# Two products on one array: moving the buffers that TensorE reads to other offsets modulo 256 bytes

## The chip, the cores and the metric

The kernel runs on one core of one Trainium2 chip. Its time is the device time of one launch in microseconds (us); the figure for the kernel before is the median of three runs. TensorE is called PE in the profile, VectorE DVE, ScalarE ACT, GpSimd POOL and SyncE SP; "PEld" is TensorE's loading of weights, which the profile lists as an engine of its own. A *pair* below is two matmuls that run at once on the two 64-row halves of TensorE's array.

## The reference

```
xn  = layernorm(x)                       # x: 2048 x 576, float32
qkv = xn @ wqkv                          # 32 heads of 18
A   = sliding dilated attention (8 keys, 2 apart) @ wo
h   = maximum(xn @ w1, 0)                # 576 -> 4608
B   = h @ w2                             # 4608 -> 576
out = x + A + B
```

All products are kept close to float32: each operand is split into a high part in the float32r format and the rest ("hi" and "lo"), and three of the four partial products are added up (hi·hi, hi·lo, lo·hi).

## The kernel before

The 2048 rows are taken in two phases of 1024, each phase in four blocks of 256 rows (NTB), and the 4608 hidden columns in 36 strips of 128, three to a chunk. One *slot* is one strip for one block, and the loop at L826 walks through 288 of them. A slot does three things on TensorE:

- **The first product** (`h_two`, L577): two slots' hidden strips are computed together, half of their terms in each of the two slots. Per slot 14 pairs of 256 columns run through `mm_rows` (L118, instruction line L125). The *weights*, the operand that is loaded into the array, are strips of the tile `w1t`; the *moving* operand, which streams through, is the transposed input `xT`. The profile names the group `ph<-xT,w1t` or `pm<-xT,w1t` by the PSUM tile that it fills.
- **q, k and v** (`qkv_tile`, L378) in 64 of the slots: 14 pairs of 432 columns, weights `xT`, moving `wq`.
- **The second product** (`o_two`, L603): 12 pairs, four sets of three. The weights are the two halves of `hhi` and `hlo`, the split hidden strip that ACT (L559) and DVE (L562) made from the first product two slots earlier; the moving operand is `w2t`, in a cut of 256 columns and one of 320 (`CUT`, L68), because one PSUM bank holds 512 columns and the product has 576. The order of a slot is 3 pairs of 256, 3 of 320, 3 of 256, 3 of 320. A set takes hi with w2's high part, hi with w2's low part, and lo with w2's high part. In eight slots the product with `wo` rides along, with weights `k` and `xn` and moving `wq` and `v`, which then hold wo.

The weights of a pair are loaded while the pair before it streams, so at nearly every moment two reads of SBUF run beside each other: the moving operand of this pair and the weights of the next.

The order of the work is written out by hand. A planner (`t["pe"]`, `t["dve"]`, L112) adds up estimated TensorE and VectorE time as instructions are issued, and `run_bg` (L498) lets attention's VectorE operations into a slot only while the VectorE estimate is not ahead. `two` (L157) makes the hi and lo parts of a weight tile: one ACT copy (L158) and one DVE subtraction (L162), with DVE's estimate raised by (columns + 70) / 960 us. The tiles of w2 are split in `w2_task` (L184) from a staging buffer `st` that SP fills by DMA.

Where a buffer lies is set by the order of the pools (L75 to L91) and their sizes: each takes the next free bytes of every partition, rounded up to 32. The first tile starts 128 bytes past a multiple of 256 in the built program. From there the offsets follow by addition: `x` is 2304 bytes, `xT` 10240, `qo` 20480, `k` and `v` 8640 each, `w1t` 5120, `w2t` 4608, `wq` 17280, `st` 2560, `hhi` and `hlo` 1024, `pr` 4608, `xn` 2560. The pool `gap` at L85 holds 192 unused bytes. The results are in the table of the section on the change.

Of the kernel before, what the change touches and what calls it, by code (L numbers as in the profile page):

```python
# [10 lines left out]
F32 = mybir.dt.float32  # L11
F32R = mybir.dt.float32r
# [6 lines left out]
P = 128  # L19
# [37 lines left out]
def tile_body(ctx: ExitStack, tc: tile.TileContext, x, wqkv, wo, w1, w2, out):  # L57
    nc = tc.nc
    S, D = x.shape
# [6 lines left out]
    DR = D - KT * P  # L66
    D2 = D // 2
    CUT = (slice(0, 256), slice(256, D))  # L68
    scale = Dh ** -0.5
    SPC = NTB * C  # L70
    SPP = NCH * SPC

    ctx.enter_context(tc.manual_schedule())
    pool = lambda name, bufs, **k: ctx.enter_context(tc.tile_pool(name=name, bufs=bufs, **k))
    consts = pool("consts", 1)  # L75
    xp = pool("xp", 11)
    xtp = pool("xtp", NTB)
# [1 line left out]
    kp = pool("kp", 1)  # L79
    vp = pool("vp", 2)  # L80
    w1p = pool("w1p", C + 1)
    w2p = pool("w2p", C + 1)
    wqp = pool("wqp", 1)
    stp = pool("stp", 5)
    gap = pool("gap", 1)  # L85
    gap.tile([P, 48], F32, name="gap")
    hp = pool("hp", LAG + 1)
    prp = pool("prp", 2)
    lgp = pool("lgp", 1)
    smp = pool("smp", 2)  # L90
    tmp = pool("tmp", 2)  # L91
    ps_o = pool("ps_o", 4, space=PSUM)
    ps_h = pool("ps_h", 2, space=PSUM)
# [20 lines left out]
    def mm(o, l, r, start, stop, n):  # L114
        nc.tensor.matmul(o, l, r, start=start, stop=stop)  # L115
        t["pe"] += n / 2400.0 + 0.002

    def mm_rows(runs, behind=None):  # L118


        if behind is not None:
            tc.add_manual_dep(nc.tensor.nop().ins, behind.ins.name, SYNC, reason="PSUM banks change rows")
        for pair in zip(*runs, strict=True):
            for z, (o, l, r, start, stop, n) in zip((slice(0, 64), slice(64, P)), pair):
                ins = nc.tensor.matmul(o, l[z], r[z], start=start, stop=stop)  # L125
            t["pe"] += pair[0][5] * 17 / 16 / 2400.0 + 0.001
        return ins

    def dve(n):
        t["dve"] += (n + 70) / 960.0  # L130
# [6 lines left out]
    def split_task(step, load, split):  # L137
        tasks.append((step, load, split))
# [18 lines left out]
    def two(hi, lo, src, n):  # L157
        nc.scalar.activation(hi, src, AF.Copy)  # L158
        if step_now in by_pool:
            nc.gpsimd.tensor_tensor(lo, src, f32(hi), op=ALU.subtract)  # L160
        else:
            nc.vector.tensor_tensor(lo, src, f32(hi), op=ALU.subtract)  # L162
            dve(n)
# [20 lines left out]
    def w2_task(step, key, f):  # L184
        def load(st):
            nc.sync.dma_start(st[:, 0:D], w2[f * P : (f + 1) * P, :])

        def split(st):
            w = w2p.tile([P, 2, D], F32R, name="w2t")
            two(w[:, 0, :], w[:, 1, :], st[:, 0:D], D)  # L190
            W2[key] = w

        split_task(step, load, split)
# [335 lines left out]
    def wo_run(ph, i, h, terms, upper):  # L529

        r, d = OT[ph, i]
        row = [r[:, j] for j in range(KT)] + [r[:, KT] if upper else d[:, KT]] + [d[:, j] for j in range(KT + 1)]
        return [(row[a], WO[ph][b][:, CUT[h]]) for a, b in terms]


    slots = [(ph, c, tb, f) for ph in range(NPH) for c in range(NCH) for tb in range(NTB) for f in range(C)]
    H, PO = {}, {}
# [60 lines left out]
    def o_tiles(n):  # L598
        for h, c in enumerate(CUT):
            for k in range(2):  # L600
                PO[k, h] = ps_o.tile([P, 512], F32, name="po")[:, 0 : c.stop - c.start]

    def o_two(n):  # L603


        ph, c, tb, f = slots[n]
        hi, lo = H.pop(n)
        w = W2[ph, c, f]
        with_wo = c == WO_CHUNK and f == C - 1
        if f == 0:  # L610
            o_tiles(n)

        def run(k, h, upper):
            cs, first = slice(k * P, (k + 1) * P), k == upper
            z = [(l[:, cs], w[:, b, CUT[h]]) for l, b in ((hi, 0), (hi, 1), (lo, 0))]
            if with_wo:
                more = wo_run(ph, 2 * tb + k, h, (UPPER_MORE if upper else LOWER_MORE) if first else (UPPER if upper else LOWER), upper)
                z = z + more
            return [
                (PO[k, h], l, r, f == 0 and first and j == 0, f == C - 1 and not first and j == len(z) - 1, CUT[h].stop - CUT[h].start)  # L620
                for j, (l, r) in enumerate(z)
            ]

        for j in range(4):
            k, h = divmod(j, 2)
            behind = PB[j - 2] if j > 1 else PB[3] if j == 0 and f else None
            PB[j] = mm_rows((run(k, h, False), run(1 - k, h, True)), behind)
        if with_wo:
            for k in range(2):
                OT.pop((ph, 2 * tb + k))  # L630
        o_out(n, rows=True)
# [3 lines left out]
    def o_mm(n, out=True, which=range(2)):  # L635
        ph, c, tb, f = slots[n]
        hi, lo = H[n]
        w = W2[ph, c, f]
        end = n == len(slots) - 1
        if f == 0 and 0 in which:  # L640
            o_tiles(n)
        for k in which:
            cs = slice(k * P, (k + 1) * P)
            terms = [(j, l, b, h) for j, (l, b) in enumerate(((hi, 0), (hi, 1), (lo, 0))) for h in range(2)]
            if end:
                terms.sort(key=lambda z: -z[3])
            for j, l, b, h in terms:
                mm(
                    PO[k, h], l[:, cs], w[:, b, CUT[h]],
                    f == 0 and j == 0, f == C - 1 and j == 2, D2,  # L650
                )
        if 1 in which:
            H.pop(n)
        if out:
            o_out(n, which)
# [4 lines left out]
    def o_out(n, which=range(2), rows=False):  # L660
        ph, c, tb, f = slots[n]
        if f < C - 1:
            return
        end = n == len(slots) - 1
        t["dve"] = max(t["dve"], t["pe"] - 0.4)
        order = [(k, h) for k in which for h in range(2)]
        if rows:
            order.sort(key=lambda z: z[1])
        elif end:
            order.sort(key=lambda z: (z[0], -z[1]))  # L670
        for k, h in order:
            i = 2 * tb + k
            acc, cols = X[ph, i], CUT[h]
            nc.vector.tensor_tensor(acc[:, cols], PO[k, h], acc[:, cols], op=ALU.add)  # L674
            dve(cols.stop - cols.start)
            if end and k:
                (nc.scalar if h else nc.sync).dma_start(o_v[ph, i][:, cols], acc[:, cols])
            elif end and h == 0:
                store(ph, i)
            elif c == NCH - 1 and h == 1 and not end:  # L680
                at(n + 1, store, ph, i)
# [15 lines left out]
    for ph in range(NPH):  # L697
        b = ph * SPP
# [16 lines left out]
        for i in range(NI):  # L715
            z = b + WO_CHUNK * SPC + C * (i // 2) + C - 1
# [67 lines left out]
    x2[1]()  # L784
    x2[3]()
    o_mm(0)
    o_mm(1)
    make_xt(0, 3, bank=ps_h)
    o_mm(2, out=False)
    stats(0, 4)  # L790
    s5 = stats(0, 5, parts=True)
# [83 lines left out]
```

## Time and profile before

| | |
|---|---|
| median of 3 runs | 1157.87 us (1157.85 to 1158.02) |
| the profiled execution's own time | 1154.82 us |
| its span, first to last instruction | 1153.0 us |
| busy PE / DVE / ACT / POOL | 1145.1 / 795.9 / 295.6 / 53.4 us |
| matmuls | 17334 |
| mean granted TensorE clock | 0.999 |

The span is what the views of the profile show; the execution's own time adds 1.8 us around it. A matmul's duration in the profile is the time from its start to its modelled end, and includes a fixed part in which the next pair is already streaming: a pair of 256 columns lasts 272 ns at the least, while a new one starts about every 113 ns. Of two matmuls of the same shape, the one with the longer duration was held up while it streamed. The views used are the page, the waits of PE, the groups of instructions by shape, the timeline, and the chain of waits.

### The profile page before, as it was taken

The page shows a single profiled execution, that of the slowest core. Times are in us where ns is not written, and L with a number is a line of the kernel's source. Part 1 is how long each engine was busy: PE and PEld are TensorE (multiplying, and loading weights), DVE is VectorE, ACT ScalarE, POOL GpSimd, SP SyncE. Part 2 cuts the span into 40 slices and gives each one's busy share as a digit, 9 for nine tenths or more (in the row PEclk, how much of TensorE's full clock was granted, in tenths as well). Part 3 has the DMA queues.
Part 4 walks back from the last instruction along what each step waited for, and adds up shares of the span by engine and source line. Part 5 has one row for each costly group of instructions (what it writes and reads, how often), then busy time and mean ns, then how long its engine had stood idle before and what let it go on. Part 6 is the DMA issues. An engine that isn't in the chain of part 4 may idle for free.

```text
span 1153.0 us, 38714 instructions
## 1 busy us (share of the span) xinstructions
PE 1145.1 (99%) x17334; PEld 1139.6 (99%) x17334; DVE 795.9 (69%) x1465; ACT 295.6 (26%) x796; POOL 53.4 (5%) x80
## 2 busy tenths in 40 slices
PE   8999999999999999999999999999999999999998
PEld 8999999999999999999999999999999999999998
DVE  7427887877788789643674179868868877896432
ACT  5322221221222221321552122222222212222110
POOL 3200000000000000000110000000000000010000
PEclk9999999999999999999999999999999999999999
DMA  6303312221221311402333033032222304122002
GB/s 186 92 25 85 85 36 66 77 63 51 63 78 32 94 33 46 140 13 56 110 101 97 2 101 87 24 87 64 59 58 53 99 2 113 55 57 76 13 2 84
DMA packets 85238, 76.75 MB, mean 67 GB/s; under 512 B 6624, under 2 KB 68832, under 8 KB 85072
## 3 DMA queue, kind: packets, MB, share of 16 engines
q1 hardware_dynamic: 84640, 73.82, 22.5%
q8 instruction: 136, 2.23, 0.8%
q10 hardware_dynamic: 432, 0.46, 0.1%
q14 instruction: 30, 0.25, 0.1%
HBM read 61.34 MB, written 4.72 MB: 57 GB/s over the span
## 4 chain that ended last, share of the span: by engine, by line
PE 97%; DVE 1%; issue 1%; DMA 1%; ACT 1%; POOL 0%; DVEq 0%; POOLq 0%; ACTq 0%
PE po L125 43%; PE pm L125 27%; PE ph L125 25%; PE pm L354 1%; PE po L115 0%; PE ph L115 0%; DMA x<-in_x 0%; DMA st<-in_w 0%; DMA st<-in_wqkv 0%; DVE bst L263 0%; POOL rstd L270 0%; DVE x L674 0%; ACT xn L283 0%; DVE w2t L162 0%; PE pm L302 0%
## 5 line engine op out<-in xcount | busy, mean ns | idle before, releaser
L125 PE MATMUL po<-w2t,hhi 64*128 64x256 f32 (+1 forms) x4448 | 447.3, 292 | 0.0
L125 PEld LDWEIGHTS po<-w2t,hhi 64*128 64x128 f32 x4448 | 357.6, 185 | 0.5
L125 PE MATMUL po<-w2t,hlo 64*128 64x256 f32 (+1 forms) x2224 | 333.6, 290 | 0.0
L125 PE MATMUL ph<-xT,w1t 64*128 64x256 f32 x5076 | 323.5, 274 | 0.0
L125 PEld LDWEIGHTS ph<-xT,w1t 64*128 64x128 f32 x5076 | 312.5, 184 | 0.1
L674 DVE TENSOR_TENSOR x<-po,x 128x320 f32<-128x320 f32 (+1 forms) x384 | 149.7, 449 | 169.1 <-PE po L125 166.4
L125 PEld LDWEIGHTS po<-w2t,hlo 64*128 64x128 f32 x2224 | 216.6, 185 | 0.0
L125 PE MATMUL pm<-wq,xT 64*128 64x432 f32 x1728 | 179.3, 354 | 0.0
L559 ACT ACTIVATE hhi<-ph 128x256 fp32r<-128x256 f32 x197 | 65.4, 381 | 418.1 <-PE ph L125 409.8
L125 PEld LDWEIGHTS pm<-wq,xT 64*128 64x128 f32 x1728 | 160.1, 184 | 3.2
L125 PE MATMUL pm<-xT,w1t 64*128 64x256 f32 x2430 | 153.5, 273 | 0.0
L125 PEld LDWEIGHTS pm<-xT,w1t 64*128 64x128 f32 x2430 | 148.4, 184 | 0.0
L562 DVE SCALAR_TENSOR_TENSOR hlo<-ph,hhi 128x256 fp32r<-128x256 f32 x197 | 74.5, 417 | 103.4 <-ACT hhi L559 103.1
L439 DVE TENSOR_TENSOR pr<-qo,k 128x1152 f32<-128x1152 f32 x64 | 85.6, 1349 | 4.2 <-DMA k<-k 4.2
L559 ACT ACTIVATE hhi<-pm 128x256 fp32r<-128x256 f32 x91 | 30.0, 382 | 222.6 <-PE pm L125 222.2
L471 DVE TENSOR_TENSOR pr<-lg,v 128x1152 f32<-128x1152 f32 x64 | 84.8, 1349 | 0.3
L442 DVE TENSOR_REDUCE lg<-pr 128x64 f32<-128x1152 f32 x64 | 84.8, 1343 | 0.0
L478 DVE TENSOR_TENSOR pr<-pr 128x288 f32<-128x288 f32 (+1 forms) x128 | 69.9, 598 | 0.0
L562 DVE SCALAR_TENSOR_TENSOR hlo<-pm,hhi 128x256 fp32r<-128x256 f32 x91 | 34.3, 418 | 37.2 <-ACT hhi L559 36.0
L162 DVE TENSOR_TENSOR w2t<-st,w2t 128x576 fp32r<-128x576 f32 x72 | 53.8, 747 | 8.8 <-ACT w2t L158 8.5
L162 DVE TENSOR_TENSOR w1t<-st,w1t 128x640 fp32r<-128x640 f32 x70 | 57.2, 817 | 3.5 <-ACT w1t L158 3.1
L406 ACT ACTIVATE k<-pm 128x144 f32<-128x144 f32 x64 | 19.3, 301 | 146.8 <-PE pm L125 119.5
(86 smaller groups left out, 710.5 us busy)
## 6 DMA issues: line engine op xcount, KB each, us to landing
st<-in_w SPq DMA_DIRECT2D x72, 288.0 KB, 3.1
st<-in_w SPq DMA_DIRECT2D x72, 256.0 KB, 3.0
st<-in_wqkv SPq DMA_DIRECT2D x32, 216.0 KB, 3.0
st<-in_w SPq DMA_DIRECT2D x144, 32.0 KB, 2.7
out<-x SPq DMA_DIRECT2D x15, 288.0 KB, 2.3
x<-in_x SPq DMA_DIRECT2D x14, 288.0 KB, 3.7
k<-k SPq DMA_DIRECT2D x8, 441.0 KB, 3.9
v<-v SPq DMA_DIRECT2D x8, 441.0 KB, 4.9
```

Source lines behind the costliest of these rows:

```text
L125: ins = nc.tensor.matmul(o, l[z], r[z], start=start, stop=stop)
L162: nc.vector.tensor_tensor(lo, src, f32(hi), op=ALU.subtract)
L354: nc.tensor.transpose(pt[:, k], src[rows, k * P : (k + 1) * P], ident[rows, rows])
L406: nc.scalar.activation(k[:, W - 1 + j, :], pq[:, 1, :], AF.Copy)
L439: nc.vector.tensor_tensor(pr[i], q, window(k, i), op=ALU.mult)
L442: nc.vector.tensor_reduce(lg[:, i], pr.pop(i).rearrange(heads, d=Dh), axis=AX.X, op=ALU.add)
L471: nc.vector.tensor_tensor(pr[i].rearrange(heads, d=Dh), e, window(v, i).rearrange(heads, d=Dh), op=ALU.mult)
L478: nc.vector.tensor_tensor(o, z[:, 0:n], z[:, n : 2 * n], op=ALU.add)
L559: nc.scalar.activation(hi, pt, AF.Relu)
L562: nc.vector.scalar_tensor_tensor(lo, pt, 0.0, f32(hi), op0=ALU.max, op1=ALU.subtract)
L674: nc.vector.tensor_tensor(acc[:, cols], PO[k, h], acc[:, cols], op=ALU.add)
```

## The change

It adds empty pools (`space`) so that some buffers move, and stores the tile `w2t` with 16 unused elements (64 bytes) between its columns 0 to 255 and its columns 256 to 575, in rows of 640 elements in place of 576. The high and the low part are therefore made by two calls of `two` per tile, one per cut. The pool `gap` goes.

```diff
+    W2CUT = (slice(0, 256), slice(272, D + 16))
...
+    def space(name, words):
+
+        pool(name, 1).tile([P, words], F32, name=name)
...
     w1p = pool("w1p", C + 1)
+    space("gap_w2", 48)
     w2p = pool("w2p", C + 1)
+    space("gap_wq", 16)
     wqp = pool("wqp", 1)
     stp = pool("stp", 5)
-    gap = pool("gap", 1)
-    gap.tile([P, 48], F32, name="gap")
+    space("gap_h", 32)
     hp = pool("hp", LAG + 1)
     prp = pool("prp", 2)
     lgp = pool("lgp", 1)
     smp = pool("smp", 2)
+    space("gap_tmp", 16)
     tmp = pool("tmp", 2)
...
-            w = w2p.tile([P, 2, D], F32R, name="w2t")
-            two(w[:, 0, :], w[:, 1, :], st[:, 0:D], D)
+            w = w2p.tile([P, 2, 640], F32R, name="w2t")
+            for z, c in zip(W2CUT, CUT):
+                two(w[:, 0, z], w[:, 1, z], st[:, c], c.stop - c.start)
             W2[key] = w
...
-            z = [(l[:, cs], w[:, b, CUT[h]]) for l, b in ((hi, 0), (hi, 1), (lo, 0))]
+            z = [(l[:, cs], w[:, b, W2CUT[h]]) for l, b in ((hi, 0), (hi, 1), (lo, 0))]
...
-                    PO[k, h], l[:, cs], w[:, b, CUT[h]],
+                    PO[k, h], l[:, cs], w[:, b, W2CUT[h]],
```

What TensorE reads, by its start in bytes modulo 256 (every strip, row and cut inside a tile starts at a multiple of 256 from the tile's start, but for the rows of `wq`, 1728 bytes apart, and the second cut of `w2t` after the change, 1088 bytes in):

| pair | moving, before | next weights in the same product, before | moving, after | next weights, after |
|---|---|---|---|---|
| first product, 256 columns | `xT` 192 | `w1t` 0 | 192 | 0 |
| second product, 256 columns | `w2t` 0 | `hhi`, `hlo` 64 | 192 | 0 |
| second product, 320 columns | `w2t` 0 | `hhi`, `hlo` 64 | 0 | 0 |
| q, k, v, 432 columns | `wq` 0, 64, 128 or 192 | `xT` 192 | as before | 192 |
| wo, 256 and 320 columns | `wq` 0 (`v` 64, 128) | `k` 192, `xn` 64 | as before | as before |

Besides these, `pr` and `lg` go from 64 to 0; `st` (128) and `xn` (64) stay where they were modulo 256.

## The prediction

> **What bounds the kernel now.** I read the page first, then who waits for whom on PE, then PE's groups by shape, then the timeline of one slot.
>
> ```profile
> span 1153.0 us, 38714 instructions
> PE 1145.1 (99%) x17334; PEld 1139.6 (99%) x17334; DVE 795.9 (69%) x1465; ACT 295.6 (26%) x796; POOL 53.4 (5%) x80
> PEclk9999999999999999999999999999999999999999
> PE 97%; DVE 1%; issue 1%; DMA 1%; ACT 1%; POOL 0%; DVEq 0%; POOLq 0%; ACTq 0%
> PE po L125 43%; PE pm L125 27%; PE ph L125 25%; PE pm L354 1%; PE po L115 0%; PE ph L115 0%; DMA x<-in_x 0%; DMA st<-in_w 0%; DMA st<-in_wqkv 0%; DVE bst L263 0%; POOL rstd L270 0%; DVE x L674 0%; ACT xn L283 0%; DVE w2t L162 0%; PE pm L302 0%
> ```
>
> TensorE is busy for all of the span, at full clock, and the chain that ended last runs through its pairs at L125, the second product (`po`) with the most, 43%. The waits of PE have five entries:
>
> ```profile
> PE po L106 <- POOL mhalf L101: 1.4, 1, 1.4
> PE pm L302 <- ACT xn L284: 1.2, 1, 1.2
> PE ph L115 <- ACT xT L307: 0.6, 1, 0.6
> PE pm L354 <- DVE xT L343: 0.4, 1, 0.4
> PE pm L302 <- DVE xT L310: 0.3, 1, 0.3
> ```
>
> That is 3.9 us in all, mostly in the start. So only two things move the time by much: how many pairs there are, which the change leaves alone, and how long a pair takes. PE's groups by shape show that this is not set by the number of columns alone (the last number before the second bar is the mean duration in ns):
>
> ```profile
> L125 PE MATMUL ph<-xT,w1t 64*128 64x256 f32 x5076 | 323.5, 274 | 0.0
> L125 PE MATMUL po<-w2t,hhi 64*128 64x320 f32 x2224 | 256.4, 306 | 0.0
> L125 PE MATMUL po<-w2t,hhi 64*128 64x256 f32 x2224 | 226.3, 278 | 0.0
> L125 PE MATMUL pm<-wq,xT 64*128 64x432 f32 x1728 | 179.3, 354 | 0.0
> L125 PE MATMUL po<-w2t,hlo 64*128 64x320 f32 x1112 | 174.3, 304 | 0.0
> L125 PE MATMUL po<-w2t,hlo 64*128 64x256 f32 x1112 | 159.3, 276 | 0.0
> L125 PE MATMUL pm<-xT,w1t 64*128 64x256 f32 x2430 | 153.5, 273 | 0.0
> L125 PE MATMUL po<-wq,k 64*128 64x320 f32 x208 | 24.6, 306 | 0.0
> L125 PE MATMUL po<-wq,k 64*128 64x256 f32 x208 | 21.0, 274 | 0.0
> L125 PE MATMUL po<-wq,xn 64*128 64x320 f32 x144 | 17.0, 305 | 0.0
> L125 PE MATMUL po<-wq,xn 64*128 64x256 f32 x144 | 14.7, 276 | 0.0
> ```
>
> With the same 256 columns the first product takes 273 to 274 ns and the second 276 to 278. For the other widths the undisturbed duration comes from the shortest ones, in the views of the tiles `w1t` and `wq` (min/median/max):
>
> ```profile
> L125 PE MATMUL ph<-xT,w1t x5076: 272/273/382, 45.1 to 1137.6; 64*128 64x256 f32 x196
> L125 PE MATMUL pm<-wq,xT x1728: 349/353/458, 40.7 to 949.8; 64*128 64x432 f32 x192
> ```
>
> (349 − 272) / (432 − 256) is 0.44 ns a column, so 320 columns should take 273 + 28 = 301 ns; they take 306 and 304. The second product's pairs are thus held up by 3 to 5 ns each: in a slot 2·(5+5+3) for the 256 cut and as much for the 320 cut, 52 ns. The timeline agrees (start and duration of each run of instructions):
>
> ```profile
> 201.46 0.39 PE L125 MATMUL po<-w2t,hhi 64*128 64x256 f32 x4
> ...
> 203.04 1.75 PE L125 MATMUL ph<-xT,w1t 64*128 64x256 f32 x28
> 204.64 0.40 PE L125 MATMUL po<-w2t,hhi 64*128 64x256 f32 x4
> ```
>
> The 14 pairs of the first product take 1.60 us from start to start, 114 ns each. Six pairs at 114 and six at 114 + 28 would make 1.54 us; the 12 of the second product take 1.58.
>
> **The change part by part.**
>
> *256 columns of the second product.* They go from moving 0 beside weights at 64 to moving 192 beside weights at 0, modulo 256. That is the place of the first product's pairs. I therefore price them with the dearer of its two rows, 274 ns, which carries what is left over when the array comes out of a disturbed second product (the 273 of `pm` carries the same). There are 2224/2 = 1112 pairs with `hhi` and 1112/2 = 556 with `hlo`: 1112 · (278 − 274) + 556 · (276 − 274) = 5.6 us less. Between the ends 0 (the offset isn't what holds them up) and 1112·5 + 556·3 = 7.2 us I take 5.6, because 7506 matmuls at this very pair of offsets run that way.
>
> *The last pair of the first product.* Beside it the first weights of h are loaded, now at 64 and then at 0. Such a pair at the end of the run before 201.46:
>
> ```profile
> L125 PE MATMUL pm<-xT,w1t 64*128 64x256 f32 x2 | 0.3, 275 | 0.0
> ```
>
> 275 against 273 in some 200 slots (those in which q, k and v do not stand between): 0.4 us less. The moving operand is `xT` at 192 in both, so this is the nearest thing to a test of the weights' place alone. Its ends are 0 and, at 4 ns a pair, 0.8.
>
> *320 columns of the second product.* They go from moving 0, weights 64 to moving 0, weights 0: the 64 bytes of room make 192 + 1088 a multiple of 256, so that both reads start at the same place. One pair of each slot already has that combination, the last one, beside which `w1t` at 0 is loaded. The one that ends the slot above (start 202.9):
>
> ```profile
> L125 PE MATMUL po<-w2t,hlo 64*128 64x320 f32 x2 | 0.3, 306 | 0.0
> ```
>
> It is held up like the rest. The wo pairs, moving 0 beside weights at 192 or 64, last 306 and 305. So with the moving read at 0, no place of the weights seen in this trace frees 320 columns, and I take no gain: 0. The ends: if all came down to 301, 1112·5 + 556·3 = 7.2 us less. On the other side stand q, k and v, whose four rows of offsets meet weights at 192. The second pair of a run has moving and weights at one place (difference 0), the eleventh a difference of 128; in the run that starts at 46.70:
>
> ```profile
> L125 PE MATMUL pm<-wq,xT 64*128 64x432 f32 x2 | 0.4, 358 | 0.0
> ...
> L125 PE MATMUL pm<-wq,xT 64*128 64x432 f32 x2 | 0.4, 360 | 0.0
> ```
>
> They lie 9 and 11 ns above the shortest, 349. With 9 ns the 320 columns would take 310: 1112·4 + 556·6 = 7.8 us more; with 11, 312: 11.1 us more. I stay at 0, since the 306 above is this width, this moving tile and this difference.
>
> *Two splits in place of one.* 72 tiles of w2 get four instructions instead of two.
>
> ```profile
> L162 DVE TENSOR_TENSOR w2t<-st,w2t 128x576 fp32r<-128x576 f32 x72 | 53.8, 747 | 8.8 <-ACT w2t L158 8.5
> L478 DVE TENSOR_TENSOR pr<-pr 128x576 f32<-128x576 f32 x64 | 45.7, 749 | 0.0
> L478 DVE TENSOR_TENSOR pr<-pr 128x288 f32<-128x288 f32 x64 | 26.5, 448 | 0.0
> L158 ACT ACTIVATE w2t<-st 128x576 fp32r<-128x576 f32 x72 | 50.0, 694 | 5.7 <-PE po L125 3.7 <-DMA st<-in_w 1.8
> L158 ACT ACTIVATE wq<-st 128x432 fp32r<-128x432 f32 x40 | 21.3, 566 | 1.1 <-DMA st<-in_wqkv 1.0
> ```
>
> DVE: (749 − 448)/288 = 1.05 ns a column gives 415 and 482 ns, 0.15 us more a tile, 10.7 us over the kernel beside its 796. ACT: (694 − 566)/144 = 0.89 gives 410 and 466, 0.18 us more a tile, 13 us beside 296. PE waits for neither after the start (the table of waits), so the cover is whole and the cost is 0. Without the cover, `hhi` and `hlo` of a slot would come 0.15 to 0.18 us late in 72 slots, 12 us; they are read one to two slots, over 1.5 us, after their product ends. The planner also counts 70/960 = 0.07 us more a tile, 5.3 us in all, and puts attention's operations somewhat later; behind them wait the L520 copies for wo, whose slots show no wait in before. No DMA is added; `st` comes free some 0.1 us later, for SP's next load, and the tile of that load is not waited for by PE in before. In the start w2's splits lie on the chain of waits (start, duration):
>
> ```profile
> 12.23 0.58 ACT w2t L158
> ...
> 12.84 0.76 DVE w2t L162
> ...
> 16.72 0.76 DVE w2t L162
> ```
>
> There a tile's last piece is ready after 410 + 466 + 482 = 1.36 us, where it was 694 + 747 = 1.44, while the next work on either engine starts 0.15 to 0.18 later: up to 0.5 us either way for the three tiles that are made there, and I take 0.
>
> *The sum:* −5.6 − 0.4 + 0 + 0 = −6.0 us. The profiled execution's own time would go from 1154.8 to 1148.8; the median of the runs lies 3.1 us above that execution, and I take the same step from it: 1157.87 − 6.0 = **1151.9 us**.
>
> **The rivals.**
>
> *Both cuts run free.* −7.2 − 7.2 − 0.4 = −14.8 us, 1143.1; with the 1 ns by which `ph` pairs lie over 273 gone as well, −2.5 more, 1140.6. For it: weights at 0 everywhere is the state in which the first product runs undisturbed, and a disturbance seems to be carried from pair to pair, so that a freed 256 cut could free its neighbour. Against it: the 306 at difference 0.
>
> *The place doesn't matter; what holds the second product up is its order.* It changes PSUM banks every three pairs, the first product once in 14. Then nothing changes but the splits: 1157.9. For it: hhi is slower than hlo at equal offsets. Against it: wo's pairs follow one another in one bank for some 15 pairs, and still show 305 and 306 at 320 columns. The Trainium skill, "TensorE: Matmul & The Clock Gate", "Step-by-step: what each phase is for", says that TensorE reads its moving operand and its weights through two independent ports and that loading the next weights takes no read bandwidth from the running matmul. By that rule this rival is the outcome. The trace speaks against the rule as far as 273 and 278 ns for equal shapes go, but no run here has yet changed a place alone.
>
> *Slower: the 320 columns collide.* Moving and weights start together at one place in 1668 pairs instead of one pair a slot. If they then behave like the worst q, k and v pair (+11 ns, 11.1 us more) while the 256 cut gains its 5.6 and the last pair 0.4, the kernel ends at 1157.87 + 11.1 − 6.0 = 1163.0; at +9 ns, 1159.7. It turns slower where the 320 pairs rise by 6.0 us / 1668 = 3.6 ns in the mean, from 305.3 to 309. Against it stands again the 306; for it, that this pair is alone in its slot and follows pairs of another offset.
>
> **How the numbers follow.** Chances: the forecast 0.35, both cuts free 0.24, the place doesn't matter 0.14, the 320 columns collide 0.27. The range reaches from the free case's 1141 to 1161.5, inside the collision, which leaves out its worst part and little else. A measurement of this kernel can tell about 0.2%, 2.3 us, from no change. Faster 0.59 (the first two), same 0.14, slower 0.27. The likeliest case's own range, with the splits' half microsecond and gains from 4 to 8 us, is 1150 to 1154.
>
> **What would show it.** Right: `po` at 256 columns falls from 278 and 276 to 273 or 274, at 320 columns it stays at 304 to 306, `ph` and `pm` stay, 12 pairs of the second product take 1.55 to 1.56 us in the timeline, and PE's waits stay under 5 us. 320 columns at 301 would show the free case, at 309 or more the collision, and all four rows as before that place doesn't matter. The forecast is wrong if PE waits for DVE or ACT in the slots (the splits), or if `xT` pairs get slower, which would mean that a disturbance is carried over.

## The result and the profile after

The changed kernel takes **1147.71 us** (median of five runs, 1147.54 to 1148.28); the kernel before, on the same chip, 1157.87 (five runs, 1157.79 to 1158.17). The ratio is 0.9913, with a 95% interval from 0.9898 to 0.9927: faster by 0.9%, 10.2 us between the medians. The forecast was 1151.9 us, 6.0 less than before; its range was 1141 to 1161.5, and the range of its likeliest case 1150 to 1154.

One thing is needed to read the numbers that follow: executions of the kernel before end at one of two levels, near 1155 and near 1158 us, and its profiled execution (1154.82) is of the lower kind. So the two profiles differ by 6.9 us (spans 1153.0 and 1146.1; the profiled execution after took 1147.92), the medians by 10.2; beside the lower level the change gains some 0.6%.

The page of the changed kernel, with its lines moved down by 9 (L125 is now L134):

```profile
span 1146.1 us, 38858 instructions
PE 1139.1 (99%) x17334; PEld 1133.3 (99%) x17334; DVE 800.2 (70%) x1537; ACT 302.5 (26%) x868; POOL 53.3 (5%) x80
PEclk9999999999999999999999999999999999999999
PE po L134 43%; PE pm L134 27%; PE ph L134 25%; PE ph L124 1%; PE po L124 1%; PE pm L364 1%; PE pm L312 0%; DMA x<-in_x 0%; DVE x L684 0%; PE pm L124 0%; ACT xn L293 0%; DVE bst L273 0%; ACT xT L317 0%; ACT xn L294 0%; DVE hlo L572 0%
```

The bound is the one of before: TensorE 99% busy with the same 17334 matmuls at full clock, and a chain that runs through the same three groups. VectorE has 72 instructions more and ScalarE 72 more. The waits of PE:

```profile
PE po L115 <- POOL mhalf L110: 1.4, 1, 1.4
PE pm L312 <- ACT xn L294: 0.6, 1, 0.6
PE ph L124 <- ACT xT L317: 0.6, 1, 0.6
PE pm L312 <- DVE xT L320: 0.4, 1, 0.4
PE pm L364 <- DVE xT L353: 0.4, 1, 0.4
```

They make 3.4 us, against 3.9. Nothing was gained or lost by waiting to speak of; what changed is how long the pairs take. PE's groups by shape (last number before the second bar: mean ns of one matmul):

```profile
L134 PE MATMUL ph<-xT,w1t 64*128 64x256 f32 x5076 | 322.1, 274 | 0.0
L134 PE MATMUL po<-w2t,hhi 64*128 64x320 f32 x2224 | 256.6, 304 | 0.0
L134 PE MATMUL po<-w2t,hhi 64*128 64x256 f32 x2224 | 225.9, 277 | 0.0
L134 PE MATMUL pm<-wq,xT 64*128 64x432 f32 x1728 | 179.3, 354 | 0.0
L134 PE MATMUL po<-w2t,hlo 64*128 64x320 f32 x1112 | 172.8, 300 | 0.0
L134 PE MATMUL po<-w2t,hlo 64*128 64x256 f32 x1112 | 158.6, 274 | 0.0
L134 PE MATMUL pm<-xT,w1t 64*128 64x256 f32 x2430 | 153.5, 273 | 0.0
```

At 256 columns `hhi` fell from 278 to 277 and `hlo` from 276 to 274; at 320 columns from 306 to 304 and from 304 to 300. The forecast was the other way round: 274 and 274 at 256, no change at 320.

A mean hides the pattern. The timeline of one slot shows it (start and duration of a run of matmuls):

```profile
202.03 1.76 PE L134 MATMUL ph<-xT,w1t 64*128 64x256 f32 x28
203.62 0.39 PE L134 MATMUL po<-w2t,hhi 64*128 64x256 f32 x4
203.85 0.28 PE L134 MATMUL po<-w2t,hlo 64*128 64x256 f32 x2
203.96 0.45 PE L134 MATMUL po<-w2t,hhi 64*128 64x320 f32 x4
204.25 0.30 PE L134 MATMUL po<-w2t,hlo 64*128 64x320 f32 x2
204.39 0.40 PE L134 MATMUL po<-w2t,hhi 64*128 64x256 f32 x4
204.62 0.28 PE L134 MATMUL po<-w2t,hlo 64*128 64x256 f32 x2
204.74 0.45 PE L134 MATMUL po<-w2t,hhi 64*128 64x320 f32 x4
...
205.17 1.08 PE L134 MATMUL ph<-xT,w1t 64*128 64x256 f32 x16
```

The 12 pairs take 205.17 − 203.62 = 1.55 us, where they took 1.58. The first set of 256 columns takes 0.34 us (203.62 to 203.96), 113 ns a pair; the second 0.35 (204.39 to 204.74). Single pairs of this slot, from the view by shape of windows that hold only them:

```profile
L134 PE MATMUL po<-w2t,hhi 64*128 64x256 f32 x1 | 0.3, 272 | 0.0
...
L134 PE MATMUL po<-w2t,hhi 64*128 64x320 f32 x2 | 0.3, 305 | 0.0
...
L134 PE MATMUL po<-w2t,hlo 64*128 64x320 f32 x2 | 0.3, 299 | 0.0
L134 PE MATMUL po<-w2t,hhi 64*128 64x256 f32 x2 | 0.3, 276 | 0.0
```

The first pair of 256 columns, which follows the first product, lasts 272 ns; the 320-column pair that follows the 256 cut 305; two pairs later, in the same set and at the same places, 299; the 256-column pair that follows the 320 cut is at 276 again. **The same pair at the same places lasts 272 or 276, depending on what ran ahead of it.**

The starts of all pairs in the trace give the account of the span. In undisturbed stretches a pair starts 113.3 ns after the one before at 256 columns, which is what the planner in `mm_rows` counts for a pair's columns (columns · 17/16 / 2400 us); held-up ones follow at 117 to 118. Taking the planner's figure away from each distance (141.7 ns at 320 columns, where the shortest distances are 140), and setting single pauses of 25 ns or more aside, leaves the *time held up*:

| after pairs of | before, us | after, us |
|---|---|---|
| second product, 256 columns | 5.87 | 3.65 |
| second product, 320 columns, next pair in the same product | 5.59 | 4.99 |
| second product, 320 columns, next pair in the first product | 1.32 | −0.08 |
| first product, last pair of the run, next in the second product | 0.82 | 0.00 |
| first product, the rest | 3.75 | 2.54 |
| q, k and v | 3.16 | 3.15 |
| all pairs of 256 columns or more | 22.37 | 15.61 |

The last row also has the pairs of wo. The total falls by 6.8 us, and the spans differ by 6.9.

### The profile page after: what moved, and what is told of

Same layout as the page of the kernel before. It is cut to its first block, busy times and chain, and to the rows that moved or that the text cites. A ratio compares the mean times of both kernels' runs of the same rounds, so it can differ in the third digit from the quotient of the medians.

```text
span 1146.1 us, 38858 instructions
## 1 busy us (share of the span) xinstructions
PE 1139.1 (99%) x17334; PEld 1133.3 (99%) x17334; DVE 800.2 (70%) x1537; ACT 302.5 (26%) x868; POOL 53.3 (5%) x80
## 4 chain that ended last, share of the span: by engine, by line
PE 98%; DVE 1%; ACT 1%; DMA 0%; issue 0%; POOL 0%; DVEq 0%; ACTq 0%
PE po L134 43%; PE pm L134 27%; PE ph L134 25%; PE ph L124 1%; PE po L124 1%; PE pm L364 1%; PE pm L312 0%; DMA x<-in_x 0%; DVE x L684 0%; PE pm L124 0%; ACT xn L293 0%; DVE bst L273 0%; ACT xT L317 0%; ACT xn L294 0%; DVE hlo L572 0%
## 5 line engine op out<-in xcount | busy, mean ns | idle before, releaser
L134 PE MATMUL po<-w2t,hhi 64*128 64x256 f32 (+1 forms) x4448 | 445.6, 291 | 0.0
L134 PEld LDWEIGHTS po<-w2t,hhi 64*128 64x128 f32 x4448 | 356.4, 184 | 0.5
L134 PE MATMUL po<-w2t,hlo 64*128 64x256 f32 (+1 forms) x2224 | 331.4, 287 | 0.0
L134 PE MATMUL ph<-xT,w1t 64*128 64x256 f32 x5076 | 322.1, 274 | 0.0
L134 PEld LDWEIGHTS ph<-xT,w1t 64*128 64x128 f32 x5076 | 310.3, 184 | 0.2
L134 PEld LDWEIGHTS po<-w2t,hlo 64*128 64x128 f32 x2224 | 216.8, 184 | 0.0
L134 PE MATMUL pm<-wq,xT 64*128 64x432 f32 x1728 | 179.3, 354 | 0.0
L134 PEld LDWEIGHTS pm<-wq,xT 64*128 64x128 f32 x1728 | 160.0, 184 | 3.3
L134 PE MATMUL pm<-xT,w1t 64*128 64x256 f32 x2430 | 153.5, 273 | 0.0
L134 PEld LDWEIGHTS pm<-xT,w1t 64*128 64x128 f32 x2430 | 148.0, 184 | 0.0
L171 DVE TENSOR_TENSOR w2t<-st,w2t 128x256 fp32r<-128x256 f32 (+1 forms) x144 | 58.8, 449 | 8.0 <-ACT w2t L167 7.9
L167 ACT ACTIVATE w2t<-st 128x256 fp32r<-128x256 f32 (+1 forms) x144 | 56.5, 449 | 4.9 <-PE po L134 3.1
```

## The experiments

Twelve kernels ran. The theories that the expectations name by letters: **D**, each pair is held up by the difference between the places of its moving operand and the next weights; **W**, what counts is that all weights lie at one place; **M**, the moving operand's place alone; **C**, a jump of place between one pair and the next costs time until it has settled; **L**, formed when the first four had run, a run of pairs is in one of two states, undisturbed (113.3 ns a pair at 256 columns) or held (117.8), and what runs ahead decides which of them it takes. Places are bytes modulo 256. All twelve compute the whole of the reference. The sums of time held up are counted as in the table above; the other figures are of the groups by shape. Each ratio is to runs of the kernel before that were made beside it; as these fell on the two levels differently (their medians go from 1155.0 to 1157.9 us), ratios that lie within 0.3% of each other are not told apart.

| run | median, us | ratio to before (95%) | ph, pm | hhi 320, 256 | held up, all / first product, us |
|---|---|---|---|---|---|
| before | | | 274, 273 | 306, 278 | 22.4 / 3.8 |
| after | 1147.71 | 0.9913 (0.9898 to 0.9927) | 274, 273 | 304, 277 | 15.6 / 2.5 |
| w_only | 1173.24 | 1.0157 (1.0141 to 1.0172) | 277, 278 | 308, 279 | 39.7 / 14.2 |
| m_only | 1166.04 | 1.0094 (1.0079 to 1.0109) | 276, 275 | 307, 279 | 33.5 / 8.9 |
| no64 | 1166.88 | 1.0102 (1.0087 to 1.0117) | 277, 277 | 306, 279 | 33.8 / 12.6 |
| same_diff | 1166.41 | 1.0098 (1.0081 to 1.0115) | 278, 278 | 304, 279 | 34.1 / 14.2 |
| split_only | 1157.49 | 1.0003 (0.9989 to 1.0016) | 275, 274 | 306, 278 | 24.2 / 5.0 |
| shift64 | 1147.62 | 0.991 (0.9886 to 0.9934) | 273, 273 | 304, 277 | 15.4 / 2.4 |
| cut64 | 1164.3 | 1.0058 (1.0037 to 1.008) | 275, 276 | 309, 278 | 24.6 / 6.6 |
| order320 | 1148.64 | 0.9918 (0.9894 to 0.9942) | 273, 273 | 306, 277 | 15.8 / 0.8 |
| wq128 | 1146.67 | 0.9915 (0.9896 to 0.9933) | 274, 273 | 304, 277 | 14.1 / 2.5 |
| wq192 | 1153.98 | 0.9972 (0.9955 to 0.9988) | 274, 274 | 305, 277 | 18.6 / 4.8 |

### One part of the move alone: w_only, m_only, no64, same_diff

**w_only** puts the weights of h to 0 and leaves `w2t` as it was (both cuts at 0, one split):

```diff
-    gap = pool("gap", 1)
-    gap.tile([P, 48], F32, name="gap")
+    space("gap_h", 32)
+    space("gap_tmp", 16)
```

> hhi and hlo at 0 modulo 256 like w1t; w2t stays where it is in before (both cuts at 0, one split per tile). Theory D (what holds a pair up is the difference of its moving operand's place and the next weights' place): the 320 cut has difference 0 as in the changed kernel, so its pairs should show 304 (hhi) and 300 (hlo) ns and bring 4.4 us; the 256 cut at difference 0 has not been seen, so 1150 to 1156 us. Theory W (what counts is that all weights lie at one place): nearly the whole gain, 1147 to 1149.5 us, with po at 256 columns at 277 and 274 ns. If the moving operand's place alone does it (theory M): no gain, 1157 to 1158.5.

**m_only** moves `w2t` alone (192 and 0, rows of 640 elements) and leaves h at 64: the diff of the change with `space("gap_h", 48)` and without `gap_tmp`.

> w2t as in the changed kernel (256 cut at 192, 320 cut at 0 modulo 256), hhi and hlo stay at 64. Theory D: the 256 cut has difference 128, the one of the last pair of the first product in before (held up by 2 to 4 ns), the 320 cut keeps 192 as in before: 1157 to 1160 us, rows near 278/276 and 306/304. Theory W: no gain, 1157 to 1159. Theory M: nearly the whole gain, 1147 to 1150.

**no64** is the changed kernel without the 64 bytes and with one split, so that the cuts of `w2t` both start at 192:

```diff
-    W2CUT = (slice(0, 256), slice(272, D + 16))
+    W2CUT = CUT
...
-            w = w2p.tile([P, 2, 640], F32R, name="w2t")
+            w = w2p.tile([P, 2, D], F32R, name="w2t")
```

> The changed kernel without the 64 bytes between the cuts and with one split per tile: weights at 0 everywhere, moving 192 for both cuts. Theory D: 256 columns as in the changed kernel (277/274 ns), 320 columns at difference 192 as in before (306/304), so 4.4 us of the gain are lost: 1151 to 1154 us. Theory W: the gain stays, 1147 to 1149. A third, C (the change of place from one pair to the next costs, since a jump of the moving operand has to settle): no jump is left between xT, the 256 and the 320 cut, so better than the changed kernel, 1141 to 1146.

**same_diff** moves the second product as a whole by 64: `w2t` at 0 and 64, h at 64. The differences between moving operand and next weights inside each product are those of the changed kernel, 192 and 0.

> The same differences in the second product as the changed kernel (192 for 256 columns, 0 for 320), at another place: hhi, hlo at 64, w2t's cuts at 0 and 64. Theory D: 1148 to 1149.5 us, po rows 277/274 and 304/300. Theory W: weights are again at two places (0 and 64), no gain, 1156 to 1159.

All four are slower than the kernel before, by 0.9% to 1.6%, and every forecast of a time missed. What they have in common lies where none of them moved anything: the first product, with `xT` at 192 and `w1t` at 0 as always. The groups by shape of w_only, then the tile `w1t` in it (ns min/median/max):

```profile
L132 PE MATMUL ph<-xT,w1t 64*128 64x256 f32 x5076 | 332.8, 277 | 0.0
L132 PE MATMUL po<-w2t,hhi 64*128 64x320 f32 x2224 | 267.0, 308 | 0.0
L132 PE MATMUL po<-w2t,hhi 64*128 64x256 f32 x2224 | 235.6, 279 | 0.0
L132 PE MATMUL po<-w2t,hlo 64*128 64x320 f32 x1112 | 182.6, 305 | 0.0
```

```profile
L132 PE MATMUL ph<-xT,w1t x5076: 272/278/387, 45.5 to 1156.0; 64*128 64x256 f32 x196
L132 PE MATMUL pm<-xT,w1t x2430: 272/278/284, 89.4 to 1162.3; 64*128 64x256 f32 x187
```

The median of the first product is 278 instead of 273. The timeline shows the pace:

```profile
102.15 1.81 PE L132 MATMUL pm<-xT,w1t 64*128 64x256 f32 x28
103.80 0.40 PE L132 MATMUL po<-w2t,hhi 64*128 64x256 f32 x4
```

14 pairs in 1.65 us, 118 ns each, against 203.62 − 202.03 = 1.59 us in the changed kernel. (A run of the first product has 14 pairs in one slot and 13 in the next; the 14 of the kernel's description hold for every other slot, and it is the same with q, k and v.) In w_only nearly all pairs of a run go at 117 to 119 ns, from the first to the last; in the changed kernel a run that follows the second product begins with 117.6, 115.9 and 114.4 ns and goes on at 113.4.

The two kinds of run lie well apart. Taking the mean distance from the fifth pair of a run on, nearly every run is below 114.5 or above 116.5 ns. Of the 269 runs that follow a set of 320 columns, the held ones (over 115.5) are 8 in before, 1 in the changed kernel, 249 in w_only, and 249 in same_diff. VectorE and ScalarE at work beside it do not explain it: in w_only these distances are 117.4 ns where VectorE is busy throughout and 117.2 where it is idle; for ScalarE they are 116.7 and 117.4.

D as stated falls with same_diff, which has the changed kernel's differences and is 1.0% slower than before. W falls with w_only, which has all weights of both products at 0 and is the slowest of all. M falls with m_only, which has the changed kernel's moving places. C, in the form that a disturbance after a jump settles, falls with the runs that do not settle. What they left is L.

m_only sharpens it. In its first 420 us all 46 runs of 13 pairs are held and all 47 runs of 14 are free. Both kinds read at the same places modulo 256 and follow a set of 320 columns at the same places, but this set runs otherwise ahead of the two: its distances are 147.4, 147.4 and 145.2 ns in the mean ahead of 13 pairs, and 158.2, 144.3 and 146.6 ahead of 14. So places and shapes alone do not settle the state, and how the pairs ahead ran goes with it; what in their course decides is not shown.

### What it isn't: split_only and shift64

**split_only** is the kernel before with two splits per tile of w2 in place of one, and no place moved (`two` called once per cut; `space("gap_h", 48)` in place of `gap`).

> The kernel before with nothing but the two splits per tile of w2 (columns 0 to 255, 256 to 575); every buffer that TensorE reads stays where it was. All theories: the splits are covered, 0 to +0.5 us against the kernel before, and TensorE's rows as before (po 278/276 and 306/304, ph 274, pm 273). If the splits or the planner's changed estimate matter by themselves: more than 2 us either way.

Its ratio is 1.0003 (0.9989 to 1.0016). The splits cost nothing that can be measured beside the upper level, as forecast. All ten of its runs are at that level (1157.16 to 1157.89), while five of the 14 runs of before made beside it are at the lower one (1154.60 to 1154.94); whether the splits keep the kernel from the lower level, some 2.7 us, is not shown. The gain of the change is not theirs in either case. In the profile after they are

```profile
L171 DVE TENSOR_TENSOR w2t<-st,w2t 128x320 fp32r<-128x320 f32 x72 | 34.8, 484 | 0.0
L167 ACT ACTIVATE w2t<-st 128x320 fp32r<-128x320 f32 x72 | 34.1, 474 | 0.0
L167 ACT ACTIVATE w2t<-st 128x256 fp32r<-128x256 f32 x72 | 30.6, 425 | 4.9 <-PE po L134 3.1 <-DMA st<-in_w 1.6
L171 DVE TENSOR_TENSOR w2t<-st,w2t 128x256 fp32r<-128x256 f32 x72 | 29.9, 415 | 8.0 <-ACT w2t L167 7.9
```

415 and 484 ns on DVE, 425 and 474 on ACT; the forecast had 415, 482, 410 and 466.

**shift64** is the changed kernel with 64 unused bytes ahead of all pools, so that every place moves by 64 and none against another:

```diff
+    space("gap_first", 16)
```

> The changed kernel with 64 unused bytes ahead of all pools, so that every buffer lies 64 bytes further and every difference stays. If only relative places count: 1147 to 1149 us and the changed kernel's rows (po 277/274 and 304/300, ph 274, pm 273). If the place modulo 256 itself counts: something else, anywhere from 1150 to 1175 by what the four kernels so far showed.

It runs like the changed kernel, 1147.62 us, with the same rows. So for this shift it is not the places themselves that matter but how the buffers lie to one another.

### Other neighbours: cut64 and order320

**cut64** puts 128 bytes between the cuts, so that the 320 columns start at 64:

```diff
-    W2CUT = (slice(0, 256), slice(272, D + 16))
+    W2CUT = (slice(0, 256), slice(288, D + 32))
```

> The changed kernel with 128 in place of 64 bytes between the cuts: the 320 cut's moving operand at 64 modulo 256, weights at 0, difference 64; all else as in the changed kernel. Theory D (each pair by its own difference): only the 320 rows change, within 300 to 310 ns, so 1146 to 1156 us, and ph and pm stay at 274 and 273. Theory L (a run of pairs settles into an undisturbed or a held state, and the pair before it decides which): the first product's rows may go to 277 or 278 with no change to its own places, which makes 1160 to 1170.

64 bytes more than in the change, and the time is 1164.3 us instead of 1147.71. The 320 columns rise to 309. Of the first product's runs behind 320 columns, 100 of 121 are held up to 550 us, and none of 134 from 600 us on. Beyond that, 116 pauses of 25 ns or more (most 50 to 75) add 7.5 us, against 0.5 in the changed kernel; they stand behind the first pair of a slot's last set, and all of them behind 520 us. So the time that L named came, but a good part of it through pauses that L does not contain. The cause of these pauses was not tried.

**order320** takes the sets of the changed kernel in the order 320, 256, 320, 256, with no place moved:

```diff
-            k, h = divmod(j, 2)
+            k, h = j // 2, 1 - j % 2
```

> The changed kernel with the sets of the second product in the order 320, 256, 320, 256 in place of 256, 320, 256, 320 (and the accumulating additions in the same order); no buffer moves. Theory D: every combination of moving place, next weights' place and width is one that the changed kernel has, with a 256 cut beside w1t at the end of the slot, so 1146 to 1149 us. Theory L: the pair ahead of the first product is another one, so its 14 pairs can settle differently: either 1146 to 1149 with ph and pm at 274 and 273, or 1158 to 1168 with them at 277 or 278.

Here the first product follows 256 columns at its own moving place, 192, and its held-up time falls from 2.5 to 0.8 us: it no longer enters held. What this gains is given back in the second product: its 256 columns now come out of 320 in both sets and are held up by 5.0 us instead of 3.6, and where the first product follows by 0.6 instead of nothing. The single pauses only change their place, from the 256 cut (2.1 us in the changed kernel, none here) to the 320 cut (0.5 there, some 2.8 here). The time is 1148.64, like the changed kernel's, as both theories allowed.

### An emptied array: drain_w and drain_a

These make the first product's pairs wait for the end of the second product in the slot before, so that the array is empty when a run begins. drain_w has w_only's places, drain_a the changed kernel's.

```diff
-            HB["ins"] = mm_rows((run(g, LOWER_MORE), run(g + 1, UPPER_MORE)))
+            HB["ins"] = mm_rows((run(g, LOWER_MORE), run(g + 1, UPPER_MORE)), PB[3])
...
-        mm_rows((run(g + 1, LOWER), run(g, UPPER)), HB["ins"])
+        mm_rows((run(g + 1, LOWER), run(g, UPPER)), PB[3] or HB["ins"])
```

> w_only with one more wait: the first pair of each slot's first product waits until the last pair of the second product in the slot before has ended, so that no first product starts out of a running pair. No place differs from w_only. The waits alone should cost about 0.17 us in each of some 280 slots, 45 to 50 us, so the time itself says little; the rows of ph and pm say it, beside those of drain_a. Theory L (the first product is either undisturbed or held, and the pair ahead of it decides): out of an emptied array the first product starts alike in this kernel and in drain_a, so ph and pm are equal in both within 1 ns, 273 to 274 each (w_only without the wait: 277 and 278), and a run of 14 pairs takes 113 ns a pair. The rival, that the places of the other buffers hold the first product by themselves, whatever ran just before: ph 277, pm 278 here, 273 in drain_a.

> The changed kernel with the same added wait as in drain_w, the control to it. Both theories: ph and pm 273 to 274 as without the wait, time 45 to 50 us above the changed kernel, 1193 to 1198 us. If an emptied array itself starts the first product in the held state, ph and pm are 277 to 278 here and in drain_w, which would also be theory L, with the held state as the one that a start from rest falls into.

The times are 1256.79 and 1248.63 us, one run each. The waits cost 0.35 us a slot rather than the 0.17 expected (0.25 from the last pair to the first, 0.1 more on that first pair); the times say nothing further. The first pair lasts up to 388 ns, which lifts the means of `ph` and `pm` to 282 in both. The medians of the tile `w1t` tell it, here of drain_w and then of drain_a:

```profile
L132 PE MATMUL ph<-xT,w1t x5076: 272/273/388, 45.6 to 1238.9; 64*128 64x256 f32 x196
L132 PE MATMUL pm<-xT,w1t x2430: 272/273/388, 91.9 to 1245.8; 64*128 64x256 f32 x187
```

```profile
L134 PE MATMUL ph<-xT,w1t x5076: 272/273/388, 45.1 to 1231.3; 64*128 64x256 f32 x196
L134 PE MATMUL pm<-xT,w1t x2430: 272/273/384, 91.4 to 1238.1; 64*128 64x256 f32 x187
```

With w_only's places and nothing else than a gap ahead of the run, the first product goes back from 278 to 273. **The places of all buffers are the same in w_only and drain_w, so the held first product was not held by where the buffers lie alone but by what ran directly ahead.** Out of the gap, the distances in drain_w behind the lengthened first one are 118.1 and 116.7 ns in the mean and come down to 113 to 115 by the fifth pair in most runs: from there the run frees itself, and from the running second product of w_only it does not. Held runs are 49 of 267 in drain_w, where w_only has 249 of 269, and 45 of 269 in drain_a, where the changed kernel has 1. So the gap does not put every run into the free state: with it, the two kernels come out nearly alike, w_only's places better and the changed kernel's worse than without. L's forecast of equal rows in both held; the means of 273 to 274 that it named did not, since the lengthened first pair had been left out.

The second product shows the other half. The groups of drain_w and then of drain_a:

```profile
L132 PE MATMUL po<-w2t,hhi 64*128 64x320 f32 x2224 | 258.8, 307 | 0.0
L132 PE MATMUL po<-w2t,hlo 64*128 64x256 f32 x1112 | 160.3, 278 | 0.0
```

```profile
L134 PE MATMUL po<-w2t,hhi 64*128 64x320 f32 x2224 | 257.5, 305 | 0.0
L134 PE MATMUL po<-w2t,hlo 64*128 64x256 f32 x1112 | 159.5, 274 | 0.0
```

Both enter it from a first product that now mostly runs free, and still w_only's places are at 307 and 278, the change's at 305 and 274. In slots without q, k and v, the first set of 256 columns goes at 119.5, 113.2 and 117.2 ns in drain_w and at 113.5, 113.4 and 113.4 in drain_a. So places do act on the pairs themselves, and their effect is then carried on.

### q, k and v: wq128 and wq192

Both lengthen the rows of `wq` to 448 elements, so that all of them lie at one place, 128 or 192, instead of four in turn.

```diff
-                    WQ[key] = wqp.tile([P, 10, 3 * UD], F32R, name="wq")
+                    WQ[key] = wqp.tile([P, 10, 448], F32R, name="wq")
```

> The changed kernel with the rows of wq made 64 bytes longer (432 to 448 columns, the last 16 unused), so that all ten rows of q, k and v's moving operand lie at 128 modulo 256 beside weights at 192; wo in the same buffer moves to 128 too. Before and after, the rows lie at 0, 64, 128 and 192 in turn, and their pairs last 354 ns against 349 to 350 undisturbed, about 3.2 us in all over 864 pairs. Theory L with the differences settling it: a difference of 192 between moving and next weights, as in both 256-column products after the change, and no change of it within the run of 14, so the run is undisturbed, wq 350 to 351, and the time 1144.5 to 1146. Its rival within L, that it is the change from one product to the next that disturbs: wq stays at 353 to 355, 1147 to 1148.5. If the product after q, k and v is tipped into the held state, ph or pm rise to 276 or more and the time to 1152 or more.

> As wq128, but with the rows of wq at 192, the place of its own weights (difference 0, the one that 320 columns have after the change), and st at 192 as well. If a difference of 0 is undisturbed like one of 192: wq 350 to 351 and 1144.5 to 1146, equal to wq128 within 1 us. If only a difference of 192 is: wq 354 or more here and 350 in wq128, 2 to 4 us between them. If neither place matters: both 1147 to 1148.5 with wq at 354.

In wq128 q, k and v's held-up time goes from 3.15 to 1.91 us (0.35 of it comes back where the second product follows), and their pairs only from 354 to 353; the second product behind them now frees itself in its first set (116.7, 115.8 and 114.2 ns a pair, in the changed kernel 117.6, 119.9 and 117.9) and goes on as behind the first product. The kernel takes 1146.67 us (1146.61 to 1146.72), between the two forecasts, and the lowest of all here. It ran on another chip than the changed kernel, beside its own runs of before, and the two ratios' intervals are nearly the same, so that it is faster than the change is not shown.

wq192, 64 bytes further, is at 1153.98 us, with seven of its nine runs between 1153.57 and 1154.31 and two at 1149.23 and 1149.28. Its rows barely tell why:

```profile
L133 PE MATMUL po<-w2t,hhi 64*128 64x320 f32 x2224 | 264.2, 305 | 0.0
L133 PE MATMUL pm<-wq,xT 64*128 64x432 f32 x1728 | 180.1, 354 | 0.0
L133 PE MATMUL po<-w2t,hlo 64*128 64x256 f32 x1112 | 166.6, 274 | 0.0
```

The mean of `hlo` at 256 columns is the changed kernel's, 274, but the group's busy time is 166.6 us against 158.6. Busy time counts a stretch in which either of a pair's two matmuls runs. With the means equal, it can grow only if the two halves of a pair start further apart: by 8.0 us / 556 pairs, 14 ns on average. The starts say when: up to some 450 us of the run, the halves of nearly every pair begin 3 ns apart, in every kernel here without the added waits; from 660 us, behind the change of phase, they begin 10 ns apart in the profiles of before and after, 37 in w_only's, 15 to 45 in wq192's, 47 to 84 in cut64's (the first product and the 256 cut), and mostly stay so for hundreds of us. In drain_w and drain_a, whose array runs empty in every slot, the most frequent distance is 3 to 4 ns in the second phase too: the gap brings the halves together again. Of wq192's 88 single pauses (3.4 us), 78 come in that second part and none before 470 us.

split_only shows the same beside the kernel before, whose places it has; its profiled execution is of the upper level, 1157.59 us. Its group of `hlo` at 256 columns:

```profile
L131 PE MATMUL po<-w2t,hlo 64*128 64x256 f32 x1112 | 164.9, 276 | 0.0
```

In before it is 159.3 us at the same 276. The windows 60 to 420 and 660 to 1020 us (length, PE busy and matmuls in them, ...) of before and then of split_only:

```profile
60.00:420.00 360.00, 360.00 (x5434) 357.24 (x5432) 271.29 (x447) 84.07 (x245) 9.20 (x10) 1.00 0.22 61
660.00:1020.00 360.00, 360.00 (x5488) 359.53 (x5487) 287.05 (x470) 86.41 (x241) 9.20 (x10) 1.00 0.23 65
```

```profile
60.00:420.00 360.00, 360.00 (x5432) 357.19 (x5432) 272.72 (x469) 86.28 (x268) 9.21 (x10) 1.00 0.22 61
660.00:1020.00 360.00, 360.00 (x5448) 360.00 (x5447) 285.91 (x488) 88.11 (x263) 9.20 (x10) 1.00 0.23 65
```

The first part runs alike, 5434 and 5432 matmuls; the second has 40 matmuls fewer in split_only, 20 pairs of some 131 ns (360 us / 2744), 2.6 us. The two spans differ by 2.8. In that part the halves of the first product's pairs start 23 ns apart in split_only and 10 in before. So the two levels of the kernel before are probably executions whose halves fell differently out of step between the phases. That is argued from one profile of each; no execution of the kernel before at 1158 us was profiled.

## Why the prediction was right, and where it was not

**The size came out near, through other terms than the forecast's.** Between the profiles it was 6.9 us for a forecast 6.0. That is luck in good part: the two largest terms were both mis-sized, in opposite directions, and the median fell outside the range of the likeliest case, between it and the rival of both cuts free (1143.1). Of the signs that the forecast had named for itself, the 12 pairs (1.55 us) and the waits (3.4 us) came; the rows of 256 columns did not fall to 273 or 274, and those of 320 did not stay.

- *256 columns of the second product, −5.6:* mis-sized; −2.2 us by the starts, and by the rows 1112·1 + 556·2 = 2.2 as well. The step that failed is the price, "the place of the first product's pairs, so 274": the pair's own two places were taken to set its duration. They do so in the first set (272 ns), which follows the first product; the third set comes out of the 320 columns and begins at 276. The row of 278 also held 23 pairs that last some 84 ns longer than the rest (1.7 ns of the mean); after the change there are 23 as well.
- *320 columns, 0:* mis-sized; by the rows 1112·2 + 556·4 = 4.4 us, by the starts 0.6 inside the product and 1.4 at its end, where the first product follows. The starts decide, as the span follows from them; why the durations fell by more is not explained. A set still begins held (305) but ends free (299), within 2 ns of the 301 that the forecast had worked out for an undisturbed pair. The argument for 0, one pair a slot at difference 0 with 306 ns, was a pair that came out of a held run: it showed the state that it came from, and not what the place alone does.
- *Last pair of the first product, −0.4:* −0.8, the upper end.
- *The first product, 0 in the sum:* −1.2 us, since it is entered from a freed 320 pair. The rival of both cuts free had this carrying over, with 2.5 us; the forecast had not.
- *The splits, 0:* right beside the upper level, by split_only.
- *The rival "320 columns collide"* is refuted: difference 0 at 320 columns gained. That the place doesn't matter is refuted by w_only, which has the instructions of the kernel before and other places, and takes 1173.24 us. The slower side of the forecast was real even so, but elsewhere. Four neighbouring placements are 0.9% to 1.6% slower than before, most of all through the first product, whose operands did not move.
- *The 10.2 us of the medians* against 6.9 of the profiles is the level of the profiled execution of before. The median of 1157.87 was 3.1 us above it, which the forecast took over as a fixed step; the changed kernel's runs stay within 0.8 us of one another, so that it did not carry over.

The Trainium skill, "SBUF — State Buffer", section "Who interferes with whom", gives TensorE one read port for the moving operand and another, independent one for the weights, and has TensorE wait for no one there. As to VectorE this case agrees, with w_only's 117.4 ns where it is busy and 117.2 where it is idle. By the rule of independent ports as the forecast used it, moving the buffers would change nothing, and the measurement decides against that: w_only, whose instructions on every engine are those of the kernel before, and whose granted clock is full as well, takes 1.0157 times as long with the same buffers at other places.

**What stays open:** the cause. The runs show that places decide and that a state is carried on; they do not show why a held run stays held in w_only and frees itself in the changed kernel. same_diff enters the first product from a second product with nearly the changed kernel's pattern, and the first product stays at 117 to 118 ns to the end. L describes this; it does not say beforehand which placement falls on which side. Whether the two reads of SBUF themselves collide, or something behind them, no run here can tell.

## What to carry to other kernels

Where a kernel is bound by TensorE and its pairs are already back to back, compare the mean of each shape with the minimum of that shape: a few ns a pair were 1% to 3% of this kernel, and moving buffers by 64 bytes or a few times that, without an instruction more, can win or lose them. Such a move has to be measured as a whole, and on the products it doesn't touch too, because a held-up state passes from one product to the next: a combination that looks good in one row, or half of a good change, can be the slowest version of all. Look at single pairs in their order before pricing a row, since a mean of 277 may be 272 and 276 taken in turn, with a few long pauses.

## What the hardware showed that was not expected

- A pair of 64-row matmuls of 256 columns has two paces, 113.3 and 117 to 118 ns, at the same places, and a run of 13 or 14 stays in the slower one throughout (249 of 269 in w_only) or leaves it after three to five pairs (all but one in after, most in drain_w).
- Only relative places counted in the one shift tried: all buffers 64 bytes further give 1147.62 us beside 1147.71.
- The two halves of the array can fall out of step, 3 ns up to some 450 us and 10 to 84 from 660 us on, and mostly stay so for hundreds of us; in split_only beside before this went with 2.6 us in 360.
